# A graph tensor product on one core: four parts of the edges instead of three, and longer blocks in the later sorting passes

## The chip, the cores and the metric

The kernel runs on one core of a Trainium2 chip. The metric is the device time of one execution in microseconds (us). The text uses the profile's names for the engines: PE (TensorE, with PEld for its weight loads), DVE (VectorE), ACT (ScalarE), POOL (GpSimd) and SP (SyncE, which here only issues DMAs).

## The reference

There are 10000 nodes with 64 channels of 4 components, and 640000 edges, each with a random source and destination. Each edge gathers its source's row, weighs it by a learned radial scalar and a small coupling tensor, and is summed into its destination; a linear mix over channels follows.

```python
N, deg, C, L, DE = 10000, 64, 64, 1, 4       # E = N * deg, M = (L + 1) ** 2 = 4
R = _silu(edge_feat @ w_rad)                              # (E, C)
xs = x[src]                                               # (E, C, M)
tp = jnp.einsum('eci,ef,ifo->eco', xs, Y, cg)             # (E, C, M)
msg = R[:, :, None] * tp
agg = _segment_sum(msg.reshape(-1, C * M), dst, N).reshape(N, C, M)
return jnp.einsum('ncm,cd->ndm', agg, w_mix)
```

## The kernel before

**Sorting instead of scattering.** The sum over destinations is done by matrix products, for which edges of nearby destinations must lie together. The kernel sorts packed records (10 words: key, Y, edge features) in two passes through DRAM. The first pass (`pass1`) puts edges into 18 groups of 576 destinations; the second (`pass2`) puts one group's records into its buckets of 32 destinations, 313 buckets in all. A tile is 128 edges, a chunk is 12 tiles. Both passes use `route`: per chunk, DVE finds slots (line 618), a slot mask (line 638), one-hot matrices (line 657, the rest of them on ACT, lines 665 and 666) and the expanded records (line 641); PE moves them (line 675), ACT evicts (line 683), and POOL stores 128 rows by one indirect DMA (line 687). Before its chunks can move, a block of chunks needs tables of destination rows (`tables`, lines 377 to 575, many small DVE instructions). In the first pass a block holds up to `p1.NC` chunks; in the second it is the whole segment, that is one group of one part.

**Parts.** The edges are cut into parts so that sorting the next part runs beside the messages of the one before. `SPLIT` lists for each part its share of the edges and how many tiles of each bucket its messages take. The tiles of a bucket add up to 17 over the parts; edges beyond a part's tiles stay in the bucket and come with the next part. Rows that do not fit into a bucket go to a spare area; 1024 slots of it are handled by `batch`, and a loop in `rest` handles more, if there are any.

**Messages.** A unit is one bucket of one part. `messages` runs a software pipeline over all units with fixed offsets between steps: POOL gathers one tile of source rows per indirect DMA (`gather`, line 1030, five units ahead, seven buffers `xg`); PE turns the edge features (`turn`, line 1043), ACT copies them (`turned`, line 1048), PE forms the radial scalars (`radial`, lines 1055 and 1056), ACT applies silu (line 1059), DVE multiplies the gathered rows by them (`products`, line 1083) and builds the selection matrices (`spots`, lines 1066 and 1069), and PE sums both into a bucket (`sums`, line 1098). In all parts but the last, ACT copies the sum and SP stores it (`evict`, lines 1127 and 1128; two buffers `Gp`). In the last part SP fetches the stored sums (`fetch`) and DVE adds them to the new one (lines 1123 and 1125, once for every earlier part); every four buckets PE mixes channels (`mix`, line 1143).

**Order.** Three generators are interleaved by hand in `groups`: the messages set the time base (four steps a unit), the first pass of the next part is spread over the units of this part and must end before its last units, and pass 2 is paced so that each segment is ready when its units come. DVE, ACT and PE run in just that order.

**Start-up.** `run` sorts part 0 alone. Into that first pass it weaves the zeroing of the DRAM regions on SP: first the buckets, then the group regions of all later parts, at 0.185 of a clear for each yield of the pass; what is left over then follows it. Part 0's own region is zeroed ahead on ACT's DMA queue.

```python
later = itertools.chain(self.clear_buckets(),
                        *(self.clear_groups(k, nc.sync) for k in range(1, len(SPLIT))))
run(weave(first, later, 0.185))
```

The constants and `run` hold the other lines that are changed:

```python
UT = 6
SPLIT = ((0.32, 5), (0.37, 6), (0.31, 6))
...
            self.p1.NC = 14
            self.p1.act = self.p2.act = 7
```

Of the kernel before, what the change touches and what calls it, by code (L numbers as in the profile page):

```python
# [22 lines left out]
AF = mybir.ActivationFunctionType  # L23
AX = mybir.AxisListType

P = 128
# [8 lines left out]
GN = B * NB  # L35
BT = 17
PT = 2 * BT - 1
UT = 6
SPLIT = ((0.32, 5), (0.37, 6), (0.31, 6))
LG = 5  # L40
LI = 8
HEAVY = 4
# [5 lines left out]
KR = 108  # L48
# [31 lines left out]
class Kernel:  # L80
    def __init__(self, ctx, tc, x, src, dst, Y, ef, w_rad, cg, w_mix, out):
# [16 lines left out]
        N, E, T, r = self.N, self.E, 12, 14  # L98
        assert N <= 127 << 7 and BT == sum(u for _, u in SPLIT) and B % 2 == 0 and HB % 2 == 0
        self.NG = (N + GN - 1) // GN  # L100
        assert self.NG <= B
        self.part, cut = [], 0
        for i, (share, _) in enumerate(SPLIT):
            end = cut + round(self.NT * share / (2 * T)) * 2 * T if i + 1 < len(SPLIT) else self.NT
            self.part.append((cut, end))
# [49 lines left out]
    def consts(self):  # L155
# [23 lines left out]
        self.i32 = self.dv[:, 0:NB]  # L179
        self.eq = self.dv[:, P:P + UT * NB].rearrange("p (t n) -> p t n", n=NB)  # L180
        self.vmsk = self.dv[:, P + UT * NB:]

# [753 lines left out]
    def messages(self):  # L936

        nc, ph = self.nc, self.ph
        units = [((k, g), j) for k, g in self.segs for j in range(self.nb(g))]
        MT, FIN = max(u for _, u in SPLIT), len(SPLIT) - 1  # L940
        n = len(units)
        IDX, XG, PRE, ST_, RT, SS, VS, GP, GS, OLD, E9, ER, SX, VX = ({} for _ in range(14))
# [81 lines left out]
        def gather(k):  # L1024
            g, j = units[k]
            si, (t0, ut) = IDX[g][0], tiles(k)
            xg = XG[k] = ph.tile([P, UT, 256], F, name="xg", bufs=LG + 2)
            for t in range(ut):
# [5 lines left out]
        def turn(k):  # L1034
            g, j = units[k]
            t0, ut = tiles(k)


            pre = PRE[k] = self.ps.tile([P, 512], F, name="pre", tag="pre", bufs=2)
            e = E9[g, j // HB].rearrange("p t h q k -> p (t h q k)")  # L1040
            b = t0 - place(g, j - j % HB)[0]
            for h, t in ((0, b), (1, b + ut - 3)):
                nc.tensor.matmul(pre[:KR, 256 + 128 * h:384 + 128 * h], e[:, 36 * t:36 * t + KR],  # L1043
                                 self.identb, start=True, stop=True)

        def turned(k):
            sT = ST_[k] = ph.tile([P, 2, P], BF, name="sT")
            nc.scalar.activation(sT[:KR].rearrange("p h e -> p (h e)"), PRE[k][:KR, 256:512], AF.Copy)  # L1048

        def radial(k):  # L1050
            ut = tiles(k)[1]
            R = RT[k] = PRE.pop(k)[:, :ut * 64]
            sT = ST_.pop(k)

            nc.tensor.matmul(R[:, :192], sT[:KR, 0], self.wr[:KR], start=True, stop=True)
            nc.tensor.matmul(R[:, 192:], sT[:KR, 1], self.wr[:KR, (6 - ut) * 64:], start=True, stop=True)  # L1056

        def silu(k):
            nc.scalar.activation(RT[k], RT[k], AF.Silu)  # L1059
# [1 line left out]
        def spots(k):  # L1061
# [5 lines left out]
                                    dl.unsqueeze(2).to_broadcast([P, ut, NB]), op=OP.is_equal)  # L1067
            S = SS[k] = ph.tile([P, UT, NB, 4], F, name="S")
            nc.vector.tensor_tensor(S[:, :ut], self.eq[:, :ut].unsqueeze(3).to_broadcast([P, ut, NB, 4]),  # L1069
# [464 lines left out]
    def run(self):  # L1534
        tile_pool, nc = self.tc.tile_pool, self.nc
        order = [self.NG - 1] + list(range(self.NG - 1))
        self.segs = [(k, g) for k in range(len(SPLIT)) for g in order]
        self.marks = [self.tc.alloc_semaphore("mark%d" % i) for i in range(2)]
        for s in self.marks:
            nc.tensor.sem_inc(s, 1)  # L1540
        with tile_pool(name="p1", bufs=2) as self.ph:
            self.rt_bufs, self.ls = 38, 8
            self.lag, self.ahead, self.early = 2, 3, 1
            self.z = self.ph.tile([P, 2048], F, name="z", bufs=1)
            nc.gpsimd.memset(self.z, 0.0)
            self.consts()

            with self.tc.manual_schedule(engines={mybir.EngineType.SP}):
                first = self.pass1(0, 8)
                next(first)  # L1550
                run(self.clear_groups(0, nc.scalar))
                for _ in range(40):
                    next(first, None)
                while self.held:
                    next(first)
                self.weights()
# [3 lines that stand above are left out]
                self.sorted = 1  # L1560
        with tile_pool(name="p2", bufs=2) as self.ph:
            self.rt_bufs, self.ls = 5, 4
            self.lag, self.ahead, self.early = 1, 2, 0
            self.p1.NC = 14
            self.p1.act = self.p2.act = 7
            with self.tc.manual_schedule(engines={mybir.EngineType.PE, mybir.EngineType.DVE,
                                                  mybir.EngineType.Activation}):
                self.groups()
        with tile_pool(name="p3", bufs=1) as self.ph:
            self.rest()  # L1570
# [29 lines left out]
```

## Time and profile before

| what | value |
|---|---|
| median of 3 runs | 8426.91 us (8418.68 to 8428.72) |
| the profiled execution, time | 8430.4 us |
| its span in the trace | 8428.6 us |
| mean granted PE clock | 0.855 |
| gathers / stores of the first pass / of pass 2 | 5165 / 417 / 489 |
| bytes moved | 1051.54 MB, 125 GB/s over the span |

Busy time is the union of an engine's instructions; issuing a DMA from SP counts as nothing, while POOL's indirect DMAs count for as long as POOL works on them. A row of a group reads: line, engine, operation, output and input by the program's names, shape, count, then busy time, the mean ns of one, and the idle time of that engine just before them with what ended it. In a row of waits the columns are the total, the number of times and the longest wait.

### The profile page before, as it was taken

Reading aid. Unit: us, or ns where it says so; the run is one execution under the profiler, and the core shown is the slowest. Engines: PE = TensorE matmul, PEld = TensorE weight load, DVE = VectorE, ACT = ScalarE, POOL = GpSimd, SP = SyncE. Lnnn points to the kernel's source line nnn. Section 1 sums busy time; section 2 is a strip of 40 time slices with the busy share of each in tenths; the row PEclk is TensorE's granted clock in tenths of the full one; section 3 lists DMA queues with packets and bytes.
Section 4 is the critical chain, followed back from the end, with each engine's and each line's share of the span. In section 5 each row is a group of like instructions: output and inputs, shape, how many; then the busy total and the mean of one; then the engine's idle time right before and its main releaser. Section 6 shows DMA issues by size and latency. Waiting matters only on the chain. (4 is left out here: it accounts for less than half of the span.)

```text
span 8428.6 us, 133579 instructions
## 1 busy us (share of the span) xinstructions
PE 5985.1 (71%) x41164; PEld 4943.4 (59%) x41164; DVE 7181.2 (85%) x14990; ACT 4614.3 (55%) x12740; POOL 5881.9 (70%) x6113
## 2 busy tenths in 40 slices
PE   5666776777767767776676676766677777778776
PEld 3334655656555656565565565555566666666666
DVE  8988999999999889988898898867787888878775
ACT  5876666666666746655565565653443443434321
POOL 1226676777767767777777777777777777777776
PEclk8977888888888879888888888887898989888888
DMA  5313343443434434444444444444455555555543
GB/s 185 112 59 96 113 117 107 118 116 112 118 110 120 119 112 129 121 122 123 120 122 124 120 119 125 116 120 121 133 147 145 145 146 145 146 148 143 146 139 114
DMA packets 691501, 1051.54 MB, mean 125 GB/s; under 512 B 268789, under 2 KB 499107, under 8 KB 690792
## 3 DMA queue, kind: packets, MB, share of 16 engines
q0 software_dynamic: 285888, 732.64, 30.5%
q1 hardware_dynamic: 402312, 301.08, 12.1%
q10 hardware_dynamic: 2592, 9.19, 0.3%
q8 instruction: 345, 5.65, 0.3%
q14 instruction: 364, 2.98, 0.1%
HBM read 841.86 MB, written 215.89 MB: 125 GB/s over the span
## 5 line engine op out<-in xcount | busy, mean ns | idle before, releaser
L1030 POOL DMA_INDIRECT xg<-in_x_dram,sidx x5165 | 4940.6, 957 | 1750.4 <-issue 1345.0
L1098 PE MATMUL G<-S,xg 128*128 128x128 f32 x20660 | 2989.8, 310 | 158.2 <-ACT Gp L1127 129.4
L1098 PEld LDWEIGHTS G<-S,xg 128*128 128x128 f32 x20660 | 2837.7, 222 | 202.2 <-ACT Gp L1127 153.3
L675 PE MATMUL pr<-X,oh 128*128 128x300 bf16 (+1 forms) x10573 | 1668.3, 312 | 548.5 <-DVE oh L657 411.4
L1083 DVE TENSOR_TENSOR xg<-xg,pre 128x1536 f32<-128x1536 f32 (+1 forms) x939 | 1516.4, 1615 | 540.3 <-DMA xg<-in_x_dram,sidx 303.3
L665 ACT ACTIVATE sq<-i,rowf 128x128 f32<-128x128 f32 x6132 | 1882.1, 391 | 11.2 <-DVE rowf L626 7.3
L641 DVE TENSOR_TENSOR X<-dv,Wt 128x1800 f32<-128x1800 f32 (+4 forms) x906 | 1741.6, 1922 | 62.1 <-PE pr L675 10.4
L675 PEld LDWEIGHTS <-oh 128*128 128x128 bf16 x10573 | 1080.1, 105 | 983.1 <-DVE oh L657 483.7
L666 ACT ACTIVATE oh<-sq,ones 128x1024 bf16<-128x1024 f32 (+3 forms) x906 | 967.1, 1067 | 27.1
L1069 DVE TENSOR_TENSOR S<-dv,pay 128x768 f32<-128x768 f32 (+1 forms) x939 | 836.7, 891 | 87.3 <-PE G L1098 29.8
L1043 PE MATMUL pre<-identb,e 128*108 128x128 bf16 x1878 | 291.2, 241 | 867.5 <-DVE xg L1083 866.6
L1043 PEld LDWEIGHTS <-e 128*108 128x108 bf16 x1878 | 236.8, 140 | 1041.1 <-issue 792.3
L1059 ACT ACTIVATE pre<-pre 128x384 f32<-128x384 f32 (+1 forms) x939 | 426.6, 454 | 716.3 <-PE pre L1056 551.0
L687 POOL DMA_INDIRECT grp<-rt,idx x417 | 420.2, 1008 | 529.0 <-ACT rt L683 196.9
L1127 ACT ACTIVATE Gp<-G 128x256 f32<-128x256 f32 x626 | 238.6, 381 | 892.0 <-PE G L1098 647.3
L687 POOL DMA_INDIRECT bkt<-rt,idx x489 | 492.7, 1008 | 224.7 <-issue 112.4
L1048 ACT ACTIVATE sT<-pre 108x256 bf16<-108x256 f32 x939 | 353.2, 376 | 527.1 <-PE pre L1043 525.2
L1143 PE MATMUL po<-wf,Gs 128*128 128x256 f32 (+2 forms) x1392 | 390.8, 443 | 184.6 <-DVE Gs L1125 184.6
L683 ACT ACTIVATE rt<-pr 128x300 bf16<-128x300 f32 (+1 forms) x906 | 358.7, 396 | 278.6 <-PE pr L678 118.5
L1143 PEld LDWEIGHTS po<-wf,Gs 128*128 128x128 f32 (+2 forms) x1392 | 282.5, 209 | 278.1 <-DVE Gs L1125 181.7
L657 DVE TENSOR_TENSOR oh<-dv,pair 128x640 bf16<-128x640 bf16 (+2 forms) x869 | 420.6, 488 | 0.3
L609 ACT ACTIVATE pc<-pp 128x432 f32<-128x432 f32 (+3 forms) x471 | 236.3, 502 | 295.5 <-DVE pos L618 227.5
(286 smaller groups left out, 6086.1 us busy)
## 6 DMA issues: line engine op xcount, KB each, us to landing
xg<-in_x_dram,sidx POOLq DMA_INDIRECT x5165
sums<-Gp SPq DMA_DIRECT2D x626, 128.0 KB
old<-sums SPq DMA_DIRECT2D x313, 256.0 KB
bkt<-z SPq DMA_DIRECT2D x26, 990.0 KB
pay<-bkt SPq DMA_DIRECT2D x68, 225.0 KB
grp<-z SPq DMA_DIRECT2D x17, 590.0 KB
Wt<-grp SPq DMA_DIRECT2D x17, 590.0 KB
ye<-in_Y_dram SPq DMA_DIRECT2D x103, 96.0 KB
```

Source lines behind the costliest of these rows:

```text
L641: nc.vector.tensor_tensor(X[:, :m, :].rearrange("p t (s w) -> p t s w", w=W), msk.unsqueeze(3).to_broadcast([P, m, ps.r, W]), QD[c // Q][1 ...
L665: nc.scalar.activation(sq[:, u, :], self.i128, AF.Square, bias=to, scale=-1.0)
L666: nc.scalar.activation(oh[:, v:v + len(at), :], sq[:, :len(at), :], AF.Relu, bias=self.ones[:, 0:1], scale=-2.0)
L675: nc.tensor.matmul(pr[:, :2 * ps.rw], oh[:, u, :], X[:, u, :].bitcast(BF), start=(u == 0), stop=(not on and u == m - 1))
L687: st = nc.gpsimd.indirect_dma_start(out=ps.dst, out_offset=bass.IndirectOffsetOnAxis(ap=idx[:, i:i + 1], axis=0), in_=RT.pop(c), in_offset ...
L1030: nc.gpsimd.indirect_dma_start(out=xg[:, t, :], out_offset=None, in_=self.x, in_offset=bass.IndirectOffsetOnAxis(ap=si[:, u:u + 1], axis=0))
L1043: nc.tensor.matmul(pre[:KR, 256 + 128 * h:384 + 128 * h], e[:, 36 * t:36 * t + KR], self.identb, start=True, stop=True)
L1059: nc.scalar.activation(RT[k], RT[k], AF.Silu)
L1069: nc.vector.tensor_tensor(S[:, :ut], self.eq[:, :ut].unsqueeze(3).to_broadcast([P, ut, NB, 4]), pb[:, :, 1:5].unsqueeze(2).to_broadcast([P ...
L1083: nc.vector.tensor_tensor(V, V, R.unsqueeze(3).to_broadcast([P, ut, 64, 4]), op=OP.mult)
L1098: nc.tensor.matmul(G[:, h].rearrange("p n f -> p (n f)"), v[:, 32 * h:32 * h + 32, :].rearrange("p c i -> p (c i)"), s.rearrange("p n f -> ...
L1143: nc.tensor.matmul(po[:nn, :256], Gs[:, h, f].rearrange("p b n -> p (b n)")[:, :nn], self.wf[:, h, f, :], start=(h + f == 0), stop=(h + f ...
```

## The change

The edges are cut into four parts of 0.20, 0.25, 0.31 and 0.24, with 3, 4, 5 and 5 tiles of a bucket. A unit has at most 5 tiles (`UT`), which makes the buffers `xg` and `S` smaller. A unit of three tiles needs only one turn, a copy of half the width and one radial product. The blocks of the first passes that run beside messages hold up to 20 chunks instead of 14. Everything that depends on the number of parts follows from `SPLIT`: the parts have 1008, 1248, 1560 and 1184 edge tiles (before: 1608, 1848 and 1544), there are 72 segments and 1252 units (before: 54 and 939), and the last part adds three stored sums instead of two.

```diff
-UT = 6
-SPLIT = ((0.32, 5), (0.37, 6), (0.31, 6))
+UT = 5
+SPLIT = ((0.2, 3), (0.25, 4), (0.31, 5), (0.24, 5))
...
-            for h, t in ((0, b), (1, b + ut - 3)):
+            for h, t in ((0, b), (1, b + ut - 3))[:1 + (ut > 3)]:
                 nc.tensor.matmul(pre[:KR, 256 + 128 * h:384 + 128 * h], e[:, 36 * t:36 * t + KR],
                                  self.identb, start=True, stop=True)
 
         def turned(k):
             sT = ST_[k] = ph.tile([P, 2, P], BF, name="sT")
-            nc.scalar.activation(sT[:KR].rearrange("p h e -> p (h e)"), PRE[k][:KR, 256:512], AF.Copy)
+            n = P if tiles(k)[1] == 3 else 2 * P
+            nc.scalar.activation(sT[:KR].rearrange("p h e -> p (h e)")[:, :n], PRE[k][:KR, 256:256 + n], AF.Copy)
...
-            nc.tensor.matmul(R[:, 192:], sT[:KR, 1], self.wr[:KR, (6 - ut) * 64:], start=True, stop=True)
+            if ut > 3:
+                nc.tensor.matmul(R[:, 192:], sT[:KR, 1], self.wr[:KR, (6 - ut) * 64:], start=True, stop=True)
...
-            self.p1.NC = 14
+            self.p1.NC = 20
```

## The prediction

> **What bounds the kernel now.** I read the page's totals first, then its forty slices, then windows cut at the stage borders, and last the waits inside each window. A stage is the time in which one part's messages are formed: stage 0 is the 313 units (one unit is one bucket of one part) of part 0, and so on. A start-up goes ahead, in which part 0 is sorted with nothing beside it.
>
> ```profile
> span 8428.6 us, 133579 instructions
> PE 5985.1 (71%) x41164; PEld 4943.4 (59%) x41164; DVE 7181.2 (85%) x14990; ACT 4614.3 (55%) x12740; POOL 5881.9 (70%) x6113
> DVE  8988999999999889988898898867787888878775
> POOL 1226676777767767777777777777777777777776
> ```
>
> VectorE looks like the bound at 85%, and POOL looks free at 70%. The windows correct both. Columns: window, its length, then busy time and count for PE, PEld, DVE, ACT, POOL, then clock, DMA share and GB/s. The first five rows are start-up, stages 0, 1 and 2, and the tail; the others are samples.
>
> ```profile
> 0.00:718.00 718.00, 417.42 (x2369) 245.21 (x2369) 646.45 (x1769) 521.05 (x1403) 188.93 (x204) 0.83 0.35 113
> 718.00:3290.00 2572.00, 1835.35 (x12751) 1507.97 (x12752) 2356.00 (x4965) 1651.26 (x4637) 1817.29 (x1882) 0.85 0.40 115
> 3290.00:6046.00 2756.00, 1897.64 (x13469) 1607.78 (x13469) 2309.01 (x4402) 1550.53 (x4271) 2092.74 (x2178) 0.84 0.42 122
> 6046.00:8378.00 2332.00, 1824.08 (x12524) 1574.26 (x12523) 1862.94 (x3844) 890.69 (x2428) 1766.09 (x1835) 0.90 0.51 145
> 8378.00:8429.00 51.00, 10.60 (x55) 8.17 (x54) 6.82 (x14) 0.76 (x2) 16.87 (x16) 0.63 0.07 21
> ...
> 100.00:550.00 450.00, 286.81 (x1738) 172.85 (x1737) 446.11 (x1034) 377.69 (x1017) 117.27 (x117) 0.87 0.37 123
> 577.00:718.00 141.00, 69.51 (x329) 38.50 (x329) 106.28 (x339) 80.45 (x219) 50.49 (x53) 0.66 0.22 62
> 718.00:2800.00 2082.00, 1496.30 (x10376) 1225.85 (x10377) 1932.83 (x4052) 1368.78 (x3836) 1466.73 (x1517) 0.85 0.40 114
> 3400.00:5400.00 2000.00, 1407.51 (x10009) 1185.05 (x10008) 1755.40 (x3349) 1189.49 (x3275) 1519.54 (x1578) 0.85 0.42 121
> ```
>
> POOL first. Its gathers take 957 ns, its stores 1008 ns, and behind nearly every one lies a gap of 0.3 us that the trace puts down to nothing but issue.
>
> ```profile
> L1030 POOL DMA_INDIRECT xg<-in_x_dram,sidx x5165 | 4940.6, 957 | 1750.4 <-issue 1345.0
> L687 POOL DMA_INDIRECT grp<-rt,idx x417 | 420.2, 1008 | 529.0 <-ACT rt L683 196.9
> L687 POOL DMA_INDIRECT bkt<-rt,idx x489 | 492.7, 1008 | 224.7 <-issue 112.4
> ...
> POOL xg L1030 <- issue: 467.3, 1534, 0.3
> ```
>
> So POOL is full at 2756/2178 = 1.265 us an instruction (stage 1) and 2332/1835 = 1.271 (stage 2, tail batch included): **stages 1 and 2 are bound by POOL**, though its busy share reads 76%. In stage 0 its 1882 instructions need only 2381 of 2572 us; there VectorE, at 1932.8/2082 = 92.8% up to 2800, sets the pace. In start-up VectorE is alone, at 446.1/450 = 99%. Two engines are close to full everywhere, and which of them is the bound changes with the stage.
>
> **The change, part by part.** (a) *Start-up.* Part 0 falls from 1608 to 1008 edge tiles, so from 134 chunks of 12 tiles to 84. The sample above holds 116 chunks (first row below: the expansions of line 641, one a chunk), or 3.85 us of VectorE a chunk.
>
> ```profile
> 100.00:550.00 450.00, 220.05 (x116) 0.87 0.37 123
> ...
> 718.00:3290.00 2572.00, 631.29 (x328) 0.85 0.40 115
> 3290.00:6046.00 2756.00, 567.47 (x291) 0.84 0.42 122
> 6046.00:8378.00 2332.00, 253.27 (x135) 0.90 0.51 145
> ```
>
> Fifty chunks fewer are 50 x 3.88 (450/116) = 194 us off. Part 0's own clearing moves 5.8 instead of 9.2 MB ahead of the first store: about 6 us. Behind the first pass, 577 to 718, the first two groups of pass 2 run nearly alone; with 9 chunks instead of 13 I take 120 us instead of 141. That makes 718 - 194 - 6 - 21 = 497.
>
> Against it stands a new wait. The zeroing of the buckets (27 yields) and of the later parts' group regions is woven into the first pass at 0.185 of its yields. Before, 27 + 36 are needed and the pass has about 388 yields left (two a chunk, about 15 and one per 40 tiles a block, less 41), so all fit. After, 27 + 54 are needed and it has about 243, room for 44; 37 clears of group regions come behind it, on SP, ahead of SP's loads for pass 2. Each such clear waits for the row store before it:
>
> ```profile
> SPq L254 <- DMA grp<-rt,idx: 172.6, 31, 9.7
> L254 SPq DMA_DIRECT2D grp<-z x36: 332/343/432, 249.6 to 501.7; - x36
> ...
> 0.00:50.00 50.00, 8.62 (x36) 4.74 (x37) 27.69 (x246) 7.71 (x21) 4.05 (x18) 1.00 0.84 283
> 100.00:150.00 50.00, 30.79 (x202) 18.86 (x200) 49.94 (x117) 44.83 (x123) 13.44 (x14) 0.93 0.63 197
> ```
>
> They carry 3,065 tiles of 5,120 bytes and one piece of part 1, 15.9 MB. At the 283 GB/s of the first 50 us that is 56 us; at 197 it is 81; if only their issue counted (37 x 0.343) it is 13. What hid them was the first pass, and that cover is gone, so I take the value of the row whose load is most like this one, 283 GB/s: start-up 497 + 57 = 554, call it 555, with ends 510 and 580.
>
> The Trainium skill, "DMA: Bandwidth & Descriptors", section "Two DMAs through the same engine are not ordered", says that descriptors of one queue start in order. By that the load for pass 2 starts behind all 37 clears, as I have it; without it, 13 us would do and the sum would fall by 44. No row here shows a load queued behind a burst.
>
> (b) *313 more units, the same gathers.* 3+4+5+5 is 17 tiles like 5+6+6, so the 5165 gathers stay. VectorE's three steps of a unit carry a fixed part, read from the two shapes:
>
> ```profile
> L1083 DVE TENSOR_TENSOR xg<-xg,pre 128x1536 f32<-128x1536 f32 x470 | 822.3, 1750 | 326.6 <-DMA xg<-in_x_dram,sidx 156.5 <-ACT pre L1059 135.1 <-issue 13.0
> L1083 DVE TENSOR_TENSOR xg<-xg,pre 128x1280 f32<-128x1280 f32 x469 | 694.1, 1480 | 213.7 <-DMA xg<-in_x_dram,sidx 146.8 <-ACT pre L1059 56.6 <-ACT e L1011 3.4
> L1069 DVE TENSOR_TENSOR S<-dv,pay 128x768 f32<-128x768 f32 x470 | 450.0, 957 | 51.9 <-PE G L1098 23.0 <-DVE dv L1066 0.5
> L1069 DVE TENSOR_TENSOR S<-dv,pay 128x640 f32<-128x640 f32 x469 | 386.7, 824 | 35.3 <-PE G L1098 6.8 <-DVE dv L1066 0.5
> L1066 DVE TENSOR_TENSOR dv<-dv,dlc 128x192 f32<-128x192 f32 x470 | 170.6, 363 | 8.5
> L1066 DVE TENSOR_TENSOR dv<-dv,dlc 128x160 f32<-128x160 f32 x469 | 156.3, 333 | 7.4
> ```
>
> A tile costs 270 + 133 + 30 = 433 ns. Each VectorE instruction overlaps its neighbour by some 40 ns (all rows added, less the busy time, over 14990), so a unit of five is 2637 - 120 = 2517 ns, of four 2084, of three 1651. The fixed part, 2517 - 5 x 433 = 352 ns, times 313 is 110 us.
>
> (c) *One more partial sum to add.* Each final unit gets a second add like this one, 426 - 40 ns, so 313 x 0.386 = 121 us of VectorE:
>
> ```profile
> L1125 DVE TENSOR_TENSOR Gs<-Gs,old 128x256 f32<-128x256 f32 x313 | 133.5, 426 | 10.7
> ```
>
> (d) *Sorting.* First passes keep 417 chunks. Pass 2 goes from 54 segments (a group of one part) to 72 and from 489 to 506 chunks; POOL gets 17 stores. The tables, from the first to the last of their lines
>
> ```profile
> L401 DVE TENSOR_TENSOR_SCAN sums<-onbkt,colsbkt 64x234 f32<-64x234 f32 x54 | 34.0, 629 | 2.0 <-ACT colsbkt L396 2.0
> L575 DVE TENSOR_TENSOR idx<-rk,dest 128x9 int32<-128x9 f32 (+6 forms) x83 | 14.3, 172 | 2.9 <-DVE pkh L792 0.4
> ```
>
> add to 908 us over 4136 instructions, 742 without overlap: some 6.4 us each for the 29 of first passes and 10.4 for the 54 of pass 2, 11.2 with the start of a segment. Eighteen more cost 202, less about 30 for shorter ones. Blocks of 20 leave 24 tables of the first passes instead of 29: 5 x 6.4 saved, some of it spent on longer rows, so about 20. The small edits (for three tiles one turn, half a copy and one radial product less) touch PE and ACT, which have room in every window; they count as nothing while ACT stays under the 64% of stage 0. The casts' remainders and the unpacking add about 35, the 17 short chunks 10.
>
> So VectorE gains about 110 + 121 + 202 - 30 - 20 + 35 + 10 = 430 us of work, while the work moved out of start-up goes to stages in which an engine is already full.
>
> **The stages afterwards.** Solving the windows of before for a chunk (stage 2 for pass 2, then stage 0 for the first pass) gives 3.0 and 4.25 us; stage 1, not used, comes out at 2291 against 2309. Then, in us of VectorE, messages + remainders and unpacking + first-pass chunks + pass 2 (0.264 a tile) + tables:
> - stage 0: 517 + 75 + 114 x 4.25 + 299 + 254 = 1630; POOL 918 + 114 + 105 = 1137 x 1.265 = 1438
> - stage 1: 652 + 77 + 130 x 4.25 + 368 + 254 = 1904; POOL 1504 x 1.265 = 1903
> - stage 2: 788 + 80 + 89 x 4.25 + 460 + 239 = 1945; POOL 1811 x 1.265 = 2291
> - stage 3: 1150 + 82 + 325 + 227 (tail included) = 1784; POOL 1538 x 1.265 = 1946
>
>
> The first-pass chunks of stage 0 include ten of the next part, as before, where 165 stores of a first pass fall into it and part 1 has 154; start-up holds 151 stores of both passes:
>
> ```profile
> 718.00:3290.00 2572.00, 166.45 (x165) 0.85 0.40 115
> ...
> 0.00:718.00 718.00, 151.52 (x151) 0.83 0.35 113
> ```
>
> VectorE can run between 92.8% (beside messages) and 99% (alone). I take 94%, nearer the first, as messages remain, but POOL has room. Stage 0 is 1630/0.94 = 1734 and stage 1 is 1904/0.94 = 2026, both **bound by VectorE**; stage 2 is POOL's 2291; stage 3 has both near full, 1960. Sum: 555 + 1734 + 2026 + 2291 + 1960 + 51 = 8617. The added work counted directly (430) is less than these stages give (about 530); half of the difference falls into stages 0 and 1 and takes off 55. I say 8600. The profiled execution took 8430.4, 3.5 above the median, which is nothing here. So 163 us won at the start, and about 335 lost: POOL's 113 more in the stages (58 stores and 14 gathers that fell into start-up, and the 17: 89 x 1.265), the rest VectorE outrunning POOL in stages 0 and 1. One part of the change stands out: a three-tile unit asks POOL for 3.8 us and VectorE for 5.2 with its share of sorting.
>
> **Rivals.**
> - *VectorE packs tighter, faster.* In start-up it reaches 99%. At 99% and with the lower count, stage 0 is (1630 - 27)/0.99 = 1619 and stage 1 is POOL's 1905, and the sum 555 + 1619 + 1905 + 2291 + 1950 + 51 = 8371; with the burst of clears at its lower end 8327. I give 8350. It decides from 97.3% up, where stages 0 and 1 take (3534 - 55)/0.973 = 3575 and the sum is 8430. For it: the row of 450 us. Against it: 2082 us beside messages at 92.8%.
> - *No change*, between the two: 8427 within 0.2%, which is about what a measurement of this kernel can tell.
> - *Stalls behind the stores of partial sums.* ACT waits for an old store when SP is held by another wait:
>
> ```profile
> ACT Gp L1127 <- DMA sums<-Gp: 177.8, 14, 26.3
> ```
>
>   Two buffers cover two units, 15 us at six tiles, 7.5 to 10 at three and four. Now POOL's queue ahead hides it; where VectorE binds, 36 segments of some 4 us more give 150: 8750.
> - *The spare area overflows.* Counting the drawn edges by the kernel's rules, 60 spare rows of pass 2 are used before and 65 after; 1024/15 = 68 fit before an extra loop runs at the end. Beyond that a loop at least as long as the tail's 51 us follows: 8655.
>
> **Chances.** My forecast 0.60, tighter packing 0.24, no change 0.06, stalls 0.08, overflow 0.02: faster 0.24, same 0.06, slower 0.70. The likeliest alone spans 8480 to 8720. The range reaches into the faster case at 8330 and to the stalls at 8770.
>
> **What would show it.** First products near 555, with the last group clears after the first pass; VectorE at 93 to 95% and POOL under 85% of its 1.265 us rate in stage 0; POOL at full rate in stage 2; VectorE's total near 7610 to 7710. I am wrong if VectorE exceeds 97% beside messages, if its total stays under 7500, or if the clears cost nothing and the stage borders hold POOL at its rate.

## The result and the profile after

The changed kernel takes 8843.51 us (8837.98 to 8845.21) against 8425.35 us (8418.68 to 8428.72) before: a ratio of 1.0496, 95% interval 1.0478 to 1.0514, or 418 us more. Forecast was 8600, range 8330 to 8770: the sign is right, the size is less than half of it, and the time lies outside the range. The chips at hand differ: on some the kernel before takes 8414 to 8428 us, on others 10,114 to 10,224 us, so every ratio below is to runs of the kernel before on the same chip, in the same set of runs; where a run is compared with after in us, the kernel before took 8424 to 8425 us on both chips.

The page of the kernel after, its totals and two of its rows of forty slices:

```profile
span 8843.4 us, 141973 instructions
PE 6188.2 (70%) x42045; PEld 5105.2 (58%) x42045; DVE 7611.9 (86%) x17538; ACT 4899.0 (55%) x14172; POOL 5917.6 (67%) x6131
DVE  9788888888888988998899888888777888888885
POOL 2156656666566766667677777777777777777775
```

VectorE gained 7611.9 - 7181.2 = 431 us of work (forecast: 430), and the kernel lost nearly the same 418. POOL's digits in the first half are now mostly sixes, with fives, where there were more sevens. The windows of after, cut at the first products of each stage: start-up, stages 0 to 3, tail. Columns as in the prediction (window, length, then PE, PEld, DVE, ACT, POOL with counts, clock, DMA share, GB/s).

```profile
0.00:516.00 516.00, 269.08 (x1524) 158.92 (x1525) 432.27 (x1333) 334.64 (x907) 119.73 (x136) 0.79 0.42 139
516.00:2364.00 1848.00, 1260.00 (x7989) 984.37 (x7989) 1622.87 (x4055) 1160.60 (x3549) 1127.65 (x1165) 0.83 0.38 107
2364.00:4468.00 2104.00, 1487.91 (x10285) 1226.40 (x10284) 1869.38 (x4183) 1335.88 (x3852) 1455.67 (x1509) 0.85 0.41 116
4468.00:6737.00 2269.00, 1586.61 (x11350) 1352.96 (x11351) 1931.80 (x3964) 1320.21 (x3739) 1723.68 (x1789) 0.85 0.43 124
6737.00:8789.00 2052.00, 1574.37 (x10842) 1374.70 (x10842) 1745.71 (x3989) 746.91 (x2124) 1474.47 (x1517) 0.90 0.57 164
8789.00:8844.00 55.00, 10.19 (x58) 7.86 (x56) 9.89 (x20) 0.76 (x2) 16.44 (x16) 0.65 0.10 29
```

| | forecast | measured | error | VectorE's work, forecast / measured | POOL, us an instruction |
|---|---|---|---|---|---|
| start-up | 555 | 516 | -39 | | |
| stage 0 | 1734 | 1848 | +114 | 1630 / 1623 | 1.586 |
| stage 1 | 2026 | 2104 | +78 | 1904 / 1869 | 1.394 |
| stage 2 | 2291 | 2269 | -22 | 1945 / 1932 | 1.268 (full) |
| stage 3 | 1960 | 2052 | +92 | 1784 / 1746 + 10 | 1.353 |
| tail | 51 | 55 | +4 | | |

The sum 8617 plus these errors is 8844. The work was forecast to within 2% in every stage. What was not forecast is how much of a stage VectorE can fill: 1623/1848 = 87.8% in stage 0, 88.8% in stage 1, 85.1% in stage 3, not 94%. Rows of the waits of after, first two in stage 0, the third in stage 1, the next two in stage 2, the last two in stage 3 (total, times, longest):

```profile
DVE xg L1085 <- ACT pre L1061: 73.7, 45, 3.6
POOL xg L1030 <- PE G L1100: 164.4, 52, 10.3
...
DVE xg L1085 <- ACT pre L1061: 75.0, 38, 4.9
...
POOL xg L1030 <- issue: 397.5, 1304, 0.3
ACT Gp L1129 <- DMA sums<-Gp: 162.2, 15, 20.8
...
DVE Gs L1125 <- PE G L1100: 204.1, 78, 4.7
POOL xg L1030 <- PE G L1100: 120.0, 26, 12.5
```

In stage 0 VectorE is idle for 225 us in pieces of a few us at most, the largest group of them behind silu on ACT (line 1061); POOL there waits for free buffers (164 us in the largest group), that is for work downstream of it, as a queue ahead of the bound does. In stage 3 two thirds of VectorE's 306 idle us are one wait: the final add on line 1125 for the bucket's sum from PE.

### The profile page after: what moved, and what is told of

The parts are those of the page before. It is cut to its first block, busy times and chain, and to the rows that moved or that the text cites. A ratio compares the mean times of both kernels' runs of the same rounds, so it can differ in the third digit from the quotient of the medians.

```text
span 8843.4 us, 141973 instructions
## 1 busy us (share of the span) xinstructions
PE 6188.2 (70%) x42045; PEld 5105.2 (58%) x42045; DVE 7611.9 (86%) x17538; ACT 4899.0 (55%) x14172; POOL 5917.6 (67%) x6131
## 5 line engine op out<-in xcount | busy, mean ns | idle before, releaser
L1100 PE MATMUL G<-S,xg 128*128 128x128 f32 x20660 | 3147.3, 316 | 233.2 <-ACT Gp L1129 184.3
L675 PE MATMUL pr<-X,oh 128*128 128x280 bf16 (+1 forms) x10590 | 1723.3, 318 | 500.6 <-DVE oh L657 311.2
L1085 DVE TENSOR_TENSOR xg<-xg,pre 128x1280 f32<-128x1280 f32 (+2 forms) x1252 | 1561.3, 1247 | 365.1 <-ACT pre L1061 292.9
L641 DVE TENSOR_TENSOR X<-dv,Wt 128x1680 f32<-128x1680 f32 (+3 forms) x923 | 1747.4, 1893 | 96.2 <-PE pr L675 43.2
L1071 DVE TENSOR_TENSOR S<-dv,pay 128x640 f32<-128x640 f32 (+2 forms) x1252 | 886.5, 708 | 136.6 <-PE G L1100 48.9
L1129 ACT ACTIVATE Gp<-G 128x256 f32<-128x256 f32 x939 | 358.5, 382 | 1028.2 <-PE G L1100 847.5
L1061 ACT ACTIVATE pre<-pre 128x320 f32<-128x320 f32 (+2 forms) x1252 | 477.4, 381 | 696.0 <-PE pre L1058 519.9
L1049 ACT ACTIVATE sT<-pre 108x256 bf16<-108x256 f32 (+1 forms) x1252 | 438.6, 350 | 563.9 <-PE pre L1043 561.9
L687 POOL DMA_INDIRECT bkt<-rt,idx x506 | 510.2, 1008 | 291.7 <-issue 103.6
L1056 PE MATMUL pre<-wr,sT 108*128 108x192 bf16 x1252 | 326.5, 261 | 255.1 <-ACT sT L1049 254.5
L1011 ACT ACTIVATE e<-er 128x240 bf16<-128x240 f32 (+7 forms) x696 | 238.8, 343 | 463.3 <-DVE er L1021 456.7
```

What stands on the lines that cost most here:

```text
L641: nc.vector.tensor_tensor(X[:, :m, :].rearrange("p t (s w) -> p t s w", w=W), msk.unsqueeze(3).to_broadcast([P, m, ps.r, W]), QD[c // Q][1 ...
L675: nc.tensor.matmul(pr[:, :2 * ps.rw], oh[:, u, :], X[:, u, :].bitcast(BF), start=(u == 0), stop=(not on and u == m - 1))
L687: st = nc.gpsimd.indirect_dma_start(out=ps.dst, out_offset=bass.IndirectOffsetOnAxis(ap=idx[:, i:i + 1], axis=0), in_=RT.pop(c), in_offset ...
L1049: nc.scalar.activation(sT[:KR].rearrange("p h e -> p (h e)")[:, :n], PRE[k][:KR, 256:256 + n], AF.Copy)
L1085: nc.vector.tensor_tensor(V, V, R.unsqueeze(3).to_broadcast([P, ut, 64, 4]), op=OP.mult)
L1100: nc.tensor.matmul(G[:, h].rearrange("p n f -> p (n f)"), v[:, 32 * h:32 * h + 32, :].rearrange("p c i -> p (c i)"), s.rearrange("p n f -> ...
```

## The experiments

The question was why 431 us of VectorE's work cost 418 us, when VectorE stood idle for some 1200 us in both kernels and POOL had looked full for two stages of three. Theory **A**: in three parts POOL, at its full rate, hides VectorE's work in stages 1 and 2; in four parts VectorE sets the pace in all stages but stage 2, and its work is paid there one for one. Rivals: the shares and their order, three tiles first, are what costs (**B**); something that comes with the units other than VectorE's work costs, such as longer waits for ACT or PE (**C**); VectorE's work is paid in full everywhere, in three parts too (**D**).

**The same work added to three parts.** Behind each product of the kernel before, VectorE reduces a constant tile, and nothing reads the result.

```diff
             nc.vector.tensor_tensor(V, V, R.unsqueeze(3).to_broadcast([P, ut, 64, 4]), op=OP.mult)
...
+            ex = ph.tile([P, 3], F, name="ex", bufs=1)
+            nc.vector.tensor_reduce(ex, self.i128[:, :112].unsqueeze(1).to_broadcast([P, 3, 112]), axis=AX.X, op=OP.max)
```

> The kernel before, three parts, with one reduction over 128 x 336 constants put on VectorE behind each unit's product: about 0.45 us net, 939 times, 420 us, as much as the fourth part added to VectorE (431). Nobody reads its result. Theory A (added work costs one for one only where VectorE binds: stage 0 of before; POOL hides it in stages 1 and 2): 140 to 200 us more than the kernel before. Theory D (VectorE's idle time does not shrink, so added work costs one for one in all stages): 380 to 430 us more.

It takes 8522.43 us against 8424.47, ratio 1.0114 (1.0094 to 1.0134): 98 us. For comparison the kernel before itself was profiled once more. That run was meant to show what is slower on the slower chips:

> The kernel before, unaltered, to have its trace from the same conditions as the runs of this study. If what is slower there is PE (pauses of its own), start-up takes the 718 us of its first profile and the three message stages are each some 20 to 25% longer, with VectorE's and POOL's busy times unchanged.

It took 8413.93 us, on a chip of the faster kind, so it says nothing of the slower ones. Windows of start-up and the three stages, first of the kernel before in that repeat, then with the added reductions, and the added group itself:

```profile
0.00:713.00 713.00, 409.52 (x2371) 243.44 (x2371) 647.37 (x1771) 521.43 (x1403) 192.35 (x204) 0.84 0.35 114
713.00:3289.00 2576.00, 1831.74 (x12782) 1505.37 (x12781) 2362.70 (x4976) 1655.94 (x4649) 1825.68 (x1891) 0.85 0.40 115
3289.00:5999.00 2710.00, 1895.40 (x13408) 1604.08 (x13407) 2292.14 (x4377) 1544.14 (x4255) 2057.39 (x2142) 0.84 0.42 122
5999.00:8358.00 2359.00, 1836.77 (x12553) 1589.61 (x12551) 1872.31 (x3852) 894.09 (x2433) 1788.79 (x1861) 0.88 0.51 145
```

```profile
717.00:3394.00 2677.00, 1857.63 (x12780) 1525.62 (x12779) 2488.42 (x5289) 1658.59 (x4648) 1826.15 (x1891) 0.84 0.39 111
3394.00:6106.00 2712.00, 1907.14 (x13410) 1614.09 (x13409) 2420.20 (x4690) 1548.76 (x4256) 2059.07 (x2144) 0.84 0.43 122
6106.00:8468.00 2362.00, 1823.09 (x12546) 1582.63 (x12545) 1994.95 (x4165) 891.63 (x2433) 1789.16 (x1860) 0.89 0.51 145
...
L1087 DVE TENSOR_REDUCE ex<-i 128x3 f32<-128x336 f32 x939 | 465.6, 496 | 0.0
```

Each stage gained 123 to 128 us of VectorE's work. Stage 0 became 101 us longer, stage 1 two, stage 2 three. D falls. A's mechanism is shown at its plainest: the same instruction costs four fifths of its time where VectorE is the bound and nothing where POOL runs at 2712/2144 = 1.265 us an instruction. The total, 98, is below the 140 to 200 that A gave: a stage's share of the added work was 126, not 140, and in stage 0 VectorE's idle time took up 25 of it (213 us in the repeat, 189 here).

**One sum less in four parts.** The third stored sum is not added in the last part, so the output lacks part 2's messages.

```diff
-                for a in range(1, FIN):
+                for a in range(1, FIN - 1):
```

> Leaves out the third stored sum in the last part (it is fetched and not added): 313 x 0.386 = 121 us less work for VectorE in stage 3. Theory A: stage 3 took 2052 us where POOL needs 1919, so 100 to 130 us less than the changed kernel's 8843. Theory B (stage 3's pace is PE and the chain of sums, not VectorE): under 40 us less.

8739.77 us, ratio 1.0375 (1.0354 to 1.0395): 104 us less than after, inside A's bounds. Its stages 2 and 3:

```profile
4469.00:6733.00 2264.00, 1579.85 (x11349) 1342.21 (x11348) 1928.36 (x3961) 1319.63 (x3739) 1719.59 (x1788) 0.85 0.44 124
6733.00:8681.00 1948.00, 1545.47 (x10835) 1350.75 (x10835) 1614.63 (x3680) 743.99 (x2124) 1462.60 (x1518) 0.92 0.61 173
```

Stage 3 has 131 us of work less and is 104 shorter; then POOL is at 1948/1518 = 1.283 us, close to full. So the work of the third add (121 us by the prediction) lies on the path, for about four fifths of it.

**Less work in the sorting.** Lines 797 to 803 join the low bits of Y and of the edge features into the tenth word of a record, with five VectorE instructions for each load of edges (105 loads); here four of the five are left out and those bits are lost, with records of the same length.

```diff
-            nc.vector.scalar_tensor_tensor(flat(b), flat(ye), SPARE, flat(hi), op0=OP.bitwise_and, op1=OP.bitwise_xor)
-            u1, u2, u3 = b[:, 0], b[:, 1, :, 0:2], b[:, 1, :, 2]
-            join = dict(op0=OP.logical_shift_right, op1=OP.bitwise_or)
-            nc.vector.scalar_tensor_tensor(u1[:, :m], b[:, 0, :m], 1, b[:, 1, :m], **join)
-            nc.vector.scalar_tensor_tensor(u2[:, :m], u1[:, :m, 0:2], 2, u1[:, :m, 2:4], **join)
-            nc.vector.scalar_tensor_tensor(u3[:, :m], u2[:, :m, 0], 4, u2[:, :m, 1], **join)
-            nc.vector.tensor_scalar(wi[:, :m, 9], u3[:, :m], 6, TAG | 255, op0=OP.logical_shift_right, op1=OP.bitwise_xor)
+            u3 = b[:, 1, :, 2]
+            nc.vector.tensor_scalar(wi[:, :m, 9], u3[:, :m], 25, TAG | 255, op0=OP.logical_shift_right, op1=OP.bitwise_xor)
```

> Leaves out four instructions of VectorE for every four chunks of the first passes (lines 797 to 802, the packing of the low bits): VectorE loses some 26 us in start-up, 40 in stage 0, 45 in stage 1 and 30 in stage 2. Theory A: start-up, stage 0 and stage 1 shorten by just that, stage 2 (POOL full) not at all, about 110 us under 8843. Theory C (a unit's chain through PE and ACT sets stages 0 and 1): start-up's 26 and little more.

8717.11 us, ratio 1.0345 (1.0325 to 1.0366): 126 us less than after, with 7611.9 - 7463.4 = 149 us less work. Start-up and the four stages:

```profile
0.00:503.00 503.00, 261.42 (x1524) 159.08 (x1525) 410.73 (x1248) 333.50 (x907) 118.58 (x136) 0.80 0.44 143
503.00:2293.00 1790.00, 1252.03 (x7989) 979.14 (x7989) 1577.26 (x3932) 1159.90 (x3549) 1124.94 (x1165) 0.83 0.39 111
2293.00:4342.00 2049.00, 1467.81 (x10286) 1214.65 (x10286) 1818.75 (x4056) 1334.56 (x3852) 1454.34 (x1510) 0.86 0.42 119
4342.00:6606.00 2264.00, 1587.37 (x11350) 1348.42 (x11349) 1898.29 (x3878) 1320.57 (x3741) 1718.90 (x1790) 0.85 0.44 125
6606.00:8660.00 2054.00, 1570.90 (x10843) 1371.91 (x10843) 1748.65 (x3989) 745.38 (x2121) 1468.12 (x1517) 0.91 0.57 164
```

In stage 0, 46 us of work less are 58 us of time, in stage 1, 51 are 55; in stage 2, 34 less are 5; stage 3 has no packing and does not move. That is A stage by stage, and it bounds VectorE's part from the other side than the first experiment did.

**Other shares.** Four tiles first and three tiles third, so that the short units stand beside another part's sorting.

```diff
-SPLIT = ((0.2, 3), (0.25, 4), (0.31, 5), (0.24, 5))
+SPLIT = ((0.275, 4), (0.302, 5), (0.208, 3), (0.215, 5))
```

> Four parts of 0.275, 0.302, 0.208 and 0.215 with 4, 5, 3 and 5 tiles: the same 1252 units, 72 segments and third add, no three-tile units in the first stage. Theory A (VectorE's work, and some 0.7 us of its idle time for each unit, are the price of a fourth part, whichever the shares): 30 more chunks of start-up, 8840 to 8950. Theory B (the three-tile first stage is out of balance between POOL and VectorE, and that is what is lost): 100 us or more come back, 8750 or less.

8771.31 us, ratio 1.0407 (1.0386 to 1.0427): 72 us less than after, below what A alone gave and above what B needed. Start-up and stages (4, 5, 3, 5 tiles):

```profile
0.00:641.00 641.00, 352.37 (x2020) 208.19 (x2020) 560.01 (x1609) 441.71 (x1193) 157.37 (x175) 0.81 0.37 121
641.00:2809.00 2168.00, 1529.94 (x10653) 1246.62 (x10652) 1963.42 (x4372) 1417.55 (x4067) 1479.22 (x1530) 0.85 0.40 114
2809.00:5083.00 2274.00, 1574.23 (x11208) 1339.23 (x11208) 1906.81 (x3943) 1280.50 (x3633) 1721.14 (x1789) 0.84 0.43 124
5083.00:6746.00 1663.00, 1156.73 (x7399) 913.52 (x7400) 1438.12 (x3627) 1035.01 (x3202) 1095.10 (x1136) 0.83 0.41 117
6746.00:8720.00 1974.00, 1548.69 (x10697) 1346.10 (x10698) 1718.43 (x3943) 705.98 (x2005) 1440.22 (x1488) 0.90 0.59 169
```

So this choice of shares takes back a sixth of the loss: its start-up is 125 us longer (641 against 516), and its four stages are 194 us shorter, with 143 us less of VectorE's work in them. It is the only other choice that was run, so how much of the rest any shares could take back is not shown. The rows also show VectorE's idle time as it is: 2168 - 1963 = 205 us at four tiles, 1663 - 1438 = 225 at three.

**The longer blocks alone.** Four parts with blocks of 14 chunks, the other half of the change undone.

```diff
-            self.p1.NC = 20
+            self.p1.NC = 14
```

> Four parts with the blocks of the later first passes back at 14 chunks. Theory A (VectorE's work is paid one for one in stages 0 and 1 of four parts): five tables of the first passes more, some 6.4 us of VectorE each less what longer rows cost, so VectorE's total rises by 15 to 30 us over 7611.9 and the time, on a chip on which the kernel before takes about 8425, is 8855 to 8880. Rival C (the longer blocks hold back pass 2 or the messages while their tables are built, and are part of the loss): 8780 or less, stages 0 and 1 shorter by 30 us or more.

8881.70 us, ratio 1.0544 (1.0527 to 1.0562): 38 us slower than after, with VectorE's total at 7662.0, 50 more. Stages 0 and 1:

```profile
519.00:2391.00 1872.00, 1269.60 (x8031) 988.57 (x8031) 1644.43 (x4161) 1162.78 (x3566) 1127.65 (x1165) 0.82 0.37 106
2391.00:4502.00 2111.00, 1487.93 (x10327) 1236.01 (x10326) 1890.47 (x4306) 1337.38 (x3862) 1457.11 (x1509) 0.85 0.41 116
```

Stage 0 pays for 22 us more work with 24 us. A gave 15 to 30 us more work and at most 8880; the work rose by more, and the time is just above. The blocks of 20 are the good part of the change, worth 38 us here; its splitting into four costs some 456, if the blocks would be worth as much in three parts, which was not run. The form of C that blames the longer blocks falls.

**The clears.** Four parts with the clears woven in at 0.4, so that they end within the first pass.

```diff
-                run(weave(first, later, 0.185))
+                run(weave(first, later, 0.4))
```

> Four parts with the clears woven into the first pass at 0.4 instead of 0.185, so that none is left behind it. If the burst of clears costs its 40 to 57 us and the woven clears hide in the pass: start-up 460 to 475, time 8790 to 8805 on a chip on which the kernel before takes about 8425. Rival: the stores of the first pass share the transfer rate with the clears and wait for them, so that the pass itself becomes longer by what the burst took: start-up 510 to 555, time 8840 to 8880.

8859.83 us, ratio 1.0521 (1.0503 to 1.0538): 16 us slower than after; products begin at 540. Two windows of this kernel within its first pass, and what POOL's stores to the group regions waited for in it:

```profile
300.00:350.00 50.00, 29.84 (x164) 17.91 (x165) 42.28 (x86) 37.28 (x99) 9.70 (x10) 0.77 0.30 108
350.00:400.00 50.00, 23.62 (x147) 14.78 (x145) 38.91 (x65) 36.46 (x97) 9.82 (x10) 0.82 0.24 85
...
POOL grp L687 <- DMA grp<-z: 122.5, 16, 47.1
```

VectorE is busy for 42 and 39 of 50 us where in after it was busy for 49.81 of the 50 us from 300 to 350, and the pass grows by more than the burst had cost: the rival's times hold. Its reason holds in part: 85 to 108 GB/s is far below the 397 that the burst itself reaches in after (below), but a store of the pass waits until a clear issued ahead of it has landed, though the two touch different rows, 122.5 us in all against this much in after:

```profile
POOL grp L687 <- DMA grp<-z: 33.2, 4, 19.0
```

**On the slower chips.** Four sets ran there, each on another chip, and their ratios differ from those above, so they are told together. No chip was used both in a set with the shorter and in one with the longer time, so that it is the chip, and not something else that differed between the sets, is not shown. The changed kernel itself:

> The changed kernel itself, unaltered, beside the kernel before and the other runs of this set, as the measure for them: if it stands to before as it did (1.050), the set is in the regime of the profile of after; if nearer to 1.02, it is in one where every engine pauses longer, and only ratios within the set are read.

10,279.3 us, ratio 1.0158 (1.0139 to 1.0176). Its totals:

```profile
span 10257.7 us, 141973 instructions
PE 6694.0 (65%) x42045; PEld 5435.9 (53%) x42045; DVE 7625.0 (74%) x17538; ACT 4913.3 (48%) x14172; POOL 5913.7 (58%) x6131
...
ACT Gp L1129 <- remote: 607.7, 146, 10.2
```

VectorE, ACT and POOL do the same work in the same time as in after, but the whole is 16% longer, PE's busy time is 506 us more, and ACT, ahead of line 1129, where it copies PE's sum, waits 608 us for a signal whose sender the trace only calls remote. The trace of after has no such wait. With VectorE at 74% one expects the experiments on its work to come out smaller, and they do. The kernel with less packing:

> Leaves out four instructions of VectorE for every four chunks of the first passes (lines 797 to 802, the packing of the low bits): 1.4 us nominal, 1.24 without overlap, for each of 104 groups of chunks, 26 us of it in start-up, 40 in stage 0, 36 in stage 1, 28 in stage 2. Theory A (VectorE's work counts one for one wherever POOL is not full): 26 + 40 + 36, about 100 us less than the changed kernel in this set. Theory C (in stages 0 and 1 the pace is a chain through PE and ACT of each unit, and VectorE waits in it anyway): start-up's 26 and little more.

10,215.67, ratio 1.0083 (1.0060 to 1.0107), 64 us less than four_again (126 on the other chips). The reductions added to three parts:

> The kernel before, three parts, with one reduction over 128 x 336 constants put on VectorE behind each unit's product: about 0.45 us net, 939 times, 420 us, as much as the fourth part added to VectorE in the two traces (431). Nobody reads its result. Theory A (added work costs one for one only where VectorE binds: stage 0 of before; POOL hides it in stages 1 and 2): 140 to 200 us more. Theory D (VectorE's idle time does not shrink, each unit brings its own stalls, so added work costs one for one in all stages): 380 to 430 us more. If PE's pauses set the pace (kernel before at 10100): under 100 us more.

10,290.64, ratio 1.0055 (1.0038 to 1.0072). The third add left out, on three chips:

> Leaves out the third stored sum in the last part (it is fetched and not added). VectorE loses 313 x 0.386 = 121 us of work in stage 3. Theory A (VectorE's work and its stalls by unit set stage 3): stage 3 falls by 100 to 120, to about 8730. Theory B (POOL's 1517 instructions x 1.265 = 1919 us set stage 3, and it was only disturbed at its border): under 40 us less.

> Leaves out the third stored sum in the last part (it is fetched and not added): 313 x 0.386 = 121 us less work for VectorE in stage 3. Theory A (VectorE's work and its stalls by unit set stage 3): 100 to 120 us less than the changed kernel in this set. Theory B (POOL's 1517 instructions x 1.265 = 1919 us set stage 3): under 40 us less.

> Leaves out the third stored sum in the last part (it is fetched and not added): 313 x 0.386 = 121 us less work for VectorE in stage 3. Where the kernel before takes 8425, as in its profile: theory A (VectorE's work and its stalls by unit set stage 3) 100 to 120 us under 8843; theory B (POOL's 1517 instructions x 1.265 = 1919 us set stage 3) under 40 us. Where the kernel before takes 10100, PE's pauses cover it and nothing changes.

10,344.81, 10,330.21 and 10,321.40; ratios 1.0221 (1.0202 to 1.0239), 1.0203 (1.0147 to 1.0258) and 1.0195 (1.0149 to 1.0241). In the second of these four_again ran on the same chip, and the median with less work is 51 us higher, with intervals that overlap: no gain is shown. The first two miss what was expected; the third had said that nothing would change on such a chip. Why the work gains nothing there is open. The remaining kernels of these sets, the silu of line 1061 left out (a step of the message, `pass` in its place):

> Leaves out the silu step (line 1061): ACT loses 1252 x 0.38 = 477 us of work and each unit's chain from the turn to the product loses one step. VectorE's work is the same. Theory A (VectorE's own work and the gaps between its dependent instructions set stages 0 and 1): at most the 74 and 75 us go that VectorE waited for silu in stages 0 and 1, and part of that comes back as other waits: 30 to 120 us less than the changed kernel in this set. Theory C (the chain of a unit through PE, ACT and VectorE, with two buffers, sets the pace): over 200 us less.

10,251.16, ratio 1.0116 (1.0090 to 1.0142): 28 us less than four_again, with intervals that touch, for a step of ACT's in each of 1252 units. There, silu's place ahead of the products explains little, though in after it ended most of VectorE's waits there; this was not repeated on the other kind of chip. The other shares, the blocks of 14 and the woven clears:

> Four parts, but of 0.275, 0.302, 0.208 and 0.215 with 4, 5, 3 and 5 tiles: the same 1252 units, 72 segments and third add, no three-tile units in the first stage. Theory A (VectorE's work, and some 0.7 us of its idle time for each unit, are the price of a fourth part, whichever the shares): 30 more chunks of start-up, 8840 to 8900. Theory B (the three-tile first stage is out of balance between POOL and VectorE, and that is what is lost): stages balance better and 100 us or more come back, 8750 or less.

> Four parts with blocks of 14 chunks, as before, in the later first passes: 31 tables of first passes instead of 24. If VectorE binds stages 0 and 1 and every microsecond of its work there counts, seven more tables of some 6.4 us cost 30 to 45: about 8880. If the longer blocks themselves hurt (longer tables that hold up the chunks), undoing them gains and the time falls under 8820.

> Four parts, the zeroing woven into the first pass at 0.4 of its yields instead of 0.185, so that all clears fit beside it. The trace of after shows the last chunks done near 365 and the loads for pass 2 issued at 411: if the burst of clears behind the first pass is a stall on the path, start-up shortens by about 40 us and the whole by as much (8800). If something else of pass 2's start takes its place, no change.

Ratios 1.0181 (1.0164 to 1.0198), 1.0217 (1.0188 to 1.0246) and 1.0206 (1.0187 to 1.0224), all above four_again's 1.0158, which comes from another chip. The medians of blocks of 14 and of woven clears are higher than after's or four_again's on both kinds of chip (for the clears on the faster kind the intervals overlap), the shares help only on one. And the kernel before without the waits of PE on a semaphore that is already set, ahead of its products for routing and for sums (lines 674 and 1096):

```diff
-        for s in self.marks:
-            self.nc.tensor.wait_ge(s, 1)
+        return
```

> The kernel before without the 5501 waits on constant semaphores that stand between PE's groups of matmuls (they are always fulfilled). If PE's supply of instructions is what pauses where the kernel before takes 10100, 12% fewer instructions on PE's queue change its time, by 100 us or more; if the pauses come from elsewhere, within 50 us of the kernel before.

10,222.1, ratio 0.9997 (0.9986 to 1.0008): taking these waits out gains nothing there.

## Why the prediction was right in sign and wrong in size

**Start-up** was right in kind: 516 for 555, near the lower end of 510. The clears did come behind the first pass. The SP queue of after (start, length, count), and the first VectorE instruction behind the pass, with the idle time before it in brackets:

```profile
298.11 109.19 SPq L254 DMA_DIRECT2D grp<-z  x45
411.65 0.81 SPq L856 DMA_DIRECT2D Wt<-grp  x2
...
411.90 0.18 DVE L866 TENSOR_SCALAR base<-bb 128x18 f32<-128x18 f32 x1 [48.70 <-DMA grp<-z]
```

Before, that change of passes took 6 us: the last expansion starts at 571.3 and lasts 1.9, and the load is issued at 579.2.

```profile
L641 DVE TENSOR_TENSOR X<-dv,Wt x134: 1874/1898/2046, 47.0 to 571.3; 128x1680 f32<-128x1680 f32 x134
...
579.20 0.81 SPq L856 DMA_DIRECT2D Wt<-grp  x2
```

So the burst cost about 48.7 - 6 = 43 us, for 57 forecast between 13 and 81. Its bytes were right and its rate was too low: 37 clears move 15.9 MB, at 397 GB/s where the term had 283, and 15.9 MB at 397 GB/s are 40 us. The window is one in the burst; the second row is the wait of the load for pass 2.

```profile
371.00:409.00 38.00, 0.00 (x0) 0.00 (x0) 0.00 (x0) 0.00 (x0) 0.00 (x0) 0.50 1.03 397
...
SPq L856 <- DMA grp<-z: 3.8, 2, 3.4
```

SP issued that load only at 411.65, after it had waited for a clear to land, and VectorE's wait ended on a clear too. The rule of the Trainium skill, "DMA: Bandwidth & Descriptors", section "Two DMAs through the same engine are not ordered", by which descriptors of one queue start in order, was therefore not put to the test: no load stood queued behind the burst. The rest of the 39 is 8 us in the first expansion, which comes 14 us earlier instead of 6, and 14 us on the way from that load to the first products, which takes 104 us where it took 139 (120 instead of 141 in the forecast's window).

**VectorE's added work** was right: 430 forecast, 431 measured, with the third add at 426 ns as in its row. The match to 1 us is partly luck: the tables (lines 340 to 580) brought about 126 us net for the 152 forecast, and the 2548 added instructions overlapped by 31 ns each, not 40.

```profile
L1127 DVE TENSOR_TENSOR Gs<-Gs,old 128x256 f32<-128x256 f32 x626 | 267.0, 426 | 21.5
```

**Stage 2 = POOL's 2291** was right: 2269, at 1.268 us an instruction. So was POOL under 85% of its rate in stage 0: 1165 x 1.265 is 1474 of 1848 us, 80%.

**The step that failed is "VectorE can run between 92.8% and 99%; I take 94%"**, in the terms of stages 0 and 1. The row it was taken from, 92.8% up to 2800, was a stage of five-tile units and a part of a window without its end; whole, that stage was 2356/2572 = 91.6%. More than that, a percentage was the wrong form. Where VectorE sets the pace it stood idle for

| stage | tiles | VectorE idle, us | for each of 313 units |
|---|---|---|---|
| before, 0 | 5 | 2572 - 2356 = 216 | 0.69 |
| with reductions, 0 | 5 | 2677 - 2488 = 189 | 0.60 |
| after, 0 | 3 | 1848 - 1623 = 225 | 0.72 |
| after, 1 | 4 | 2104 - 1869 = 235 | 0.75 |
| less packing, 0 and 1 | 3, 4 | 213 and 230 | 0.68, 0.74 |
| other shares, 0 and 2 | 4, 3 | 205 and 225 | 0.65, 0.72 |

whether the stage lasts 1663 or 2677 us. With the 216 us of before, stage 0 would have been 1623 + 216 = 1839 and stage 1 2085, within 19 us of what was measured; at 91.6% they would have been 1772 and 2040. So shorter stages didn't shrink the idle time, and a fourth stage adds it once more.

That it belongs to the unit is not shown: every stage has the same 313 units, so an amount for each unit and one for each stage give the same numbers. Summed by line, the idle time also changes its place. In stage 0 of before 87 of 216 us lie ahead of the messages' lines (1000 to 1299), in stages 0 and 1 of after 133 of 225 and 131 of 235; the rest lies ahead of the sorting's lines and fell from 129 to 92 and 104. That the sum stays near 0.7 us a unit is in part a coincidence of the two. What causes either part was not settled; silu ended 74 and 75 us of it.

**Stage 3 = 1960 with both near full** failed too, by 92: there VectorE was idle for 306 us, 0.98 a unit, two thirds of it in the final add's wait for PE's sum, and POOL was at 1.353 us. The sum left 176 us for VectorE beside its work of 1784 and had no term for this wait. It isn't new with the third add. It stood in the last stage of before, where POOL was full, and it stands in the run with one add less:

```profile
DVE Gs L1123 <- PE G L1098: 146.8, 62, 4.2
...
DVE Gs L1125 <- PE G L1100: 195.4, 81, 4.0
```

What paid was the add's work: without it the stage takes 1948, close to POOL's rate and to the 1960 that had been forecast with the add in it. No run took the wait away, so what it costs by itself is open.

**The 55 us taken off**, because the direct count of the added work (430) was lower than the stages' (530), had a sound reason. Measured, VectorE's work in stages and tail rose by 645 us, the 431 and 214 moved out of start-up, where the stages' sums had it rise by 728 (the 530, and some 198 moved); in stages 0 and 1 the work came out 42 us below them, which at 94% are 45 us of time. But 8617 - 55 is 8562, not the 8600 that was said. The 38 us between them are small beside the 244 that the forecast missed.

**The rivals.** Tighter packing asked for 97.3% and got 88%. Stalls behind the stores of partial sums: ACT waited 162 us for them, but in stage 2, where POOL was full; in stages 0 and 1 it was 1 and 15 us, so they don't explain the 114 and 78 there. The spare area didn't overflow: the tail is 55 us.

Why the kernel lost can then be read from two sums over the message stages. Before, VectorE's 6528 plus 3 x 216 of idle is 7176, less than POOL's 5895 x 1.265 = 7457: POOL's floor, and VectorE's work partly free, as the reductions showed. After, VectorE's 7170 plus 4 x 216 is 8034, more than POOL's 5980 x 1.265 = 7565. By these sums the bound of the message stages as a whole went from POOL to VectorE, and of VectorE's rise of 858, 642 are work and 216 the idle time of one more stage, a cost of the kind that rival C named. By the same sums (an estimate) even perfectly matched stages would end at 516 + 8034 + 55 = 8605, above before. That 418 lies so near 431 is a coincidence of several terms: start-up fell by 202 us, and the stages rose by 613, with 642 more work and 29 less idle time of VectorE. No version tried was faster than the kernel before by more than the noise.

The Trainium skill's "Perfetto Trace Analysis", section "Identifying Performance Opportunities", names the engine with the highest occupancy as the most contended, to be worked on first. For the kernel before that is VectorE at 85%, POOL having 70%. The run with reductions speaks against that in two stages of three: 380 us of more work on that engine cost 98 in all, because POOL, busy for 76% of stages 1 and 2, was full. For the changed kernel the rule fits: 149 us less of VectorE's work, at 86%, gave 126.

## What to carry to other kernels

Price the idle time of the engine that sets the pace as an amount, taken from a whole stage in which that engine is the bound, and not as a percentage: here it was 189 to 235 us a stage, whether the stage was long or short. That one more stage pays it once more is read from these rows; units and stages were not varied apart. Before adding work to an engine, find what hides it, stage by stage; a cheap probe is to add a known amount of useless work to that engine and look which stages become longer. A wait that costs nothing while another engine is full may come to count when that engine no longer is; the wait for PE's sum stood in the last stage of both kernels. A split that shortens a serial start-up (here by 202 us) pays for its tables, its extra adds and its extra units on the engine that becomes the bound, and the sum of work plus idle time per engine over the whole run can show that before any stage is worked out.

## What the runs showed of the hardware

POOL's instructions, nearly all of them indirect DMAs of 128 rows, took 1.265 us each on average where POOL set the pace (2712 us for 2144 of them with the reductions added), though each kept POOL busy for only about 1 us: an engine that reads 76% busy was full.

The same program took 8843.4 us of span on one chip and 10,257.7 on another, with VectorE's, ACT's and POOL's busy times within 0.3%, a granted clock of 0.853 and 0.806, and start-up nearly the same (516 and 529 us); the message stages carry the difference. The slower trace has waits for a sender that it only calls remote, the largest (608 us) for PE's sums on line 1129. Leaving out PE's waits on semaphores already set changed nothing in the kernel before (0.9997). What is slower there is open. The kernel before differs by 20% between the two kinds of sets, four times the effect of this change, so only comparisons within one set mean anything here.
